# Retention on one NeuronCore: chunks of 64 tokens on 64x64 array tiles in place of chunks of 128, with the states formed one excursion ahead

## The chip, the cores and the metric

The kernel runs on one NeuronCore of a Trainium2 chip. The metric is the device time of one launch in microseconds. TensorE multiplies (a stationary operand is loaded, a moving one streams through a 128x128 array, and the result lands in PSUM), VectorE and ScalarE work on elements, GpSimd (POOL) and SyncE (SP) here mostly issue DMA transfers. Engines run side by side and wait for each other by semaphores; each works through its own instructions in order.

## The reference

Three stages follow each other. Retention is causal attention without softmax: for 8 batches, 8 heads, 576 tokens and 64 dimensions

```python
scores = scale * np.matmul(q, k.transpose(0, 1, 3, 2))
Dmat = np.where(rel >= 0, gamma[:, None, None] ** rel[None, :, :], 0.0)
return np.matmul(scores * Dmat[None], v)
```

where `rel` is the query's position less the key's and `gamma` is a constant per head. The heads are then joined to 4608 tokens of 512 features. The first expert layer ("moe") computes `((x @ w1) * (x @ w2)) @ w3 @ w_out`, the second ("moe2") computes `h = x @ w_in`, `g = h * clip(h + 3, 0, 6) / 6` and `g @ w_out`.

## The kernel before

**Products.** The expert layers use fp32r operands split into a high and a low part, three matmuls for each product (`mm3`, lines 124 to 128). The retention products and the product `w3 @ w_out` are plain fp32 matmuls; the trace shows each of these as two passes, with two weight loads and two matmuls. 

**Order.** The program is written as one long list of TensorE work, and everything else is put into it by slots: `at(s, f)` files a function under slot `s`, and `tick()`, called once before each `mm3` (or each weights product in the prologue), runs what is filed under the present slot. So the order of every queue, SP's and POOL's DMA issues among them, is the order of slots. `LEAD` is 14 slots, `B0 = LEAD + 64` is the first slot of the first expert layer, `SPB` = 96 slots is one block of 512 tokens there, and `E0` is the first slot of its last block.

**Stages.** The prologue (line 462 on) forms `W = w3 @ w_out` in 64 matmuls while SP loads the weights, whose 64-bit words VectorE and ScalarE turn into fp32 (`weights`, line 133). Then nine blocks `ffn1(j)` (line 497) compute the first expert layer: `pa`, `pb`, their product `ab`, and `px` from `ab` and `W`. Their output is stored to DRAM (`xod`) as the operands of a Strassen-like scheme, and the weights of moe2 are prepared meanwhile and stored to `wid` and `wqd` (`job`, line 608). In the second part `run_set` (line 744) multiplies `xod` operands by eight weight sets `wset` and writes the gated result to `gd`, and `out_block` (line 902) multiplies sums of `gd` blocks (`s_sum`, `prep`) by `wqd` weights and stores the output.

**Retention.** Its 36 tiles of 128 tokens (two heads side by side on the partitions, four head pairs) are woven into the prologue and the `ffn1` blocks as excursions: at slot `ex[t]` TensorE leaves the expert layer and runs `excursion(t)` (line 294): the scores of tile t+1, then for tile t the product of the queries with the state (`cross`), masked scores times values (`pv`), and this tile's addition to the state (`state`). A sequence is 4.5 tiles, so t % 9 decides where a state starts or ends: with t % 9 == 0 there is no cross product, with 4 it covers 64 queries, and with 8 no state is formed.

- `scores` (209): 16 matmuls on 64x64 array tiles, each with 64 keys as stationary operand; 8 stream 128 queries and 8 the later 64 alone.
- `cross` (225): 8 matmuls on 64x64 array tiles, 128 queries streamed (64 where t % 9 == 4), into the PSUM tile `z`.
- `pv` (240): 8 matmuls with 128 keys on the rows and 64 columns, 128 queries streamed, added to `z`.
- `state` (250): 8 matmuls with 128 keys on the rows and 64 columns, 64 streamed.

After it, at `ex[t] + 1`, VectorE scales the result (`x_out`, 270), adds the state to `S` in SBUF (`s_add`, 263) and masks the next scores (`p_mask`, 217, two instructions, one of two masks); `x_hi` and `x_lo` follow at +2 and +3, with `v_scale(t+1)` (200), and POOL issues `load_kv(t+2)` (194, three transfers) and `load_qk(t+3)`. A `kv` tile's buffer is one of two, and is filled again when `pv` and `state` have read it.

**The join.** In the last `ffn1` block SP loads operands (`load_xop`, 653) and the first weight sets (`load_set`, 642) into space that the first layer has left: sets 0, 1 and 2 at slots `E0` + 62, 76 and 88, set 3 at +105, after the last stores of `xod` (`x2_store`, 591, on SP in this block).

Of the kernel before, what the change touches and what calls it, by code (L numbers as in the profile page):

```python
# [26 lines left out]
def retention_moe_kernel(  # L27
# [54 lines left out]
    wqd = dram_p.tile([7, NSET, 128, 2, 256], F32, name="wqd")  # L82
# [125 lines left out]

    def scores(t):
        c = tiles[t]  # L210
        for a in range(2):
            for g, jh in ((0, 0), (0, 1), (1, 0), (1, 1)):
                for b, rows in enumerate(HALF):
                    nc.tensor.matmul(out=sc[HALF[jh ^ g], b, 2 * g + a, 64 * jh:128], lhsT=c["kT"][rows, g, a, HALF[jh]],  # L214
                                     rhs=c["q"][rows, g, a, 64 * jh:128], start=True, stop=True, skip_group_check=True)

    def p_mask(t):
        c = tiles[t]
        c["P"] = pl_p.tile([128, 2, NPAIR, 128], F32, tag="P", name="P")
        m = mask[:, 1 if t % PER == 4 else 0].rearrange("p g (o i) -> p g o i", o=1).to_broadcast([128, 2, 2, 128])  # L220
        for b in range(2):
            nc.vector.tensor_tensor(out=c["P"][:, b].rearrange("p (g a) i -> p g a i", g=2),
                                    in0=sc[:, b].rearrange("p (g a) i -> p g a i", g=2), in1=m, op=ALU.mult)

    def cross(t):
        c = tiles[t]
        zs = ps_z.tile([128, 2, 512], F32, tag="z", name="z")
        c["z"] = z = zs[:, :, 0:256].rearrange("p b (g i) -> p b g i", g=2)
        c["st"] = zs[:, :, 256:384].rearrange("p g (a e) -> p g a e", a=2)
        r = t % PER  # L230
        c["ni"] = ni = 0 if r == 0 else (64 if r == 4 else 128)
        if not ni:
            return
        for g in range(2):
            for a, cols in enumerate(HALF):
                for b, rows in enumerate(HALF):
                    nc.tensor.matmul(out=z[cols, b, g, 0:ni], lhsT=S[rows, 1 - g, a, :], rhs=c["q"][rows, g, a, 0:ni],
                                     start=g == 0, stop=False, skip_group_check=True)

    def pv(t):  # L240
        c = tiles[t]
        for g in range(2):
            for b in range(2):
                for a, cols in enumerate(HALF):
                    d = slice(128 * b + 64 * a, 128 * b + 64 * a + 64)
                    nc.tensor.matmul(out=c["z"][cols, b, g, :], lhsT=c["v"][:, g, d], rhs=c["P"][:, b, 2 * g + a, :],  # L246
                                     start=not c["ni"] and g == 0, stop=True, skip_group_check=True)


    def state(t):  # L250
        r = t % PER
        if r == 8:
            return
        c = tiles[t]
        for g in range(2):
            rows = HALF[1 - g] if r == 4 else slice(0, 128)
            for a in range(2):
                for b, cols in enumerate(HALF):
                    d = slice(128 * b + 64 * a, 128 * b + 64 * a + 64)
                    nc.tensor.matmul(out=c["st"][cols, 1 - g, a, :], lhsT=c["k"][rows, g, d], rhs=c["v"][rows, g, d],  # L260
                                     start=False, stop=True, skip_group_check=True)

    def s_add(t):
        c = tiles[t]
        if t % PER in (0, 4):
            nc.vector.tensor_copy(out=S, in_=c["st"])
        elif t % PER != 8:
            nc.vector.tensor_tensor(out=S, in0=S, in1=c["st"], op=ALU.add)

    def x_out(t):  # L270
# [3 lines left out]
        for a in range(0, 128, min(128, SEQ - off)):  # L274
            n, m = min(128, SEQ - off), (off + a) % SEQ // 64
            for p in range(NPAIR):
                nc.vector.scalar_tensor_tensor(
                    out=c["x32"][:, p, a:a + n], in0=c["z"][:, p % 2, p // 2, a:a + n], scalar=cw[:, m, p:p + 1],
# [27 lines left out]
    with tc.manual_schedule():  # L306
# [20 lines left out]
        mask = tb_p.tile([128, 2, 2, 128], F32, name="mask")  # L327
        sc = ps_sc.tile([128, 2, NPAIR, 128], F32, name="sc")
        nc.vector.memset(sc, 0.0)
        rate = tb_p.tile([128, PER, 8], F32, name="rate")  # L330
        cw = tb_p.tile([128, PER, NPAIR], F32, name="cw")
        S = tb_p.tile([128, 2, 2, 64], F32, name="S")
# [19 lines left out]
        mt = ut_p.tile([128, 2, 128], F32, name="mt")  # L352

        def load_tables():
            nc.vector.memset(g64[:, 0:1], 0.0)
            nc.gpsimd.dma_start(out=g64, in_=rates[64, 0:8].partition_broadcast(128))
            for g, rows, js in ((0, slice(0, 128), slice(0, 128)), (1, A, Bh), (1, Bh, A)):
                nc.gpsimd.dma_start(out=mt[rows, g], in_=tables[js, 0, 1, 0])
                nc.gpsimd.dma_start(out=back[rows, 4 * g:4 * g + 4], in_=rates[js, 4 * g:4 * g + 4])
# [662 lines left out]
```

## Time and profile before

| | |
|---|---|
| runs before (3) | 1465.98 us median, 1464.68 to 1471.44 |
| the profiled execution's own time | 1472.47 us |
| its span, first to last instruction | 1470.7 us |
| instructions | 24250 |
| busy share PE, DVE, ACT, POOL | 99%, 68%, 39%, 17% |
| DMA | 287.22 MB, mean 195 GB/s |

The profile is of one execution. PE is TensorE's matmuls, PEld its weight loads, DVE VectorE, ACT ScalarE; a name such as `z<-P,kv` gives the tile written and the tiles read, and L246 is line 246. Matmuls overlap, so a row's duration is longer than the time by which it moves the next one; the starts tell that.

### The profile page before, as it was taken

To read this page: it belongs to the slowest core of one execution; us is meant where nothing else is said; L and a number is where in the kernel's file an instruction comes from. 1 tells how busy PE (TensorE), PEld (TensorE's weight loads), DVE (VectorE), ACT (ScalarE), POOL (GpSimd) and SP (SyncE) were. 2 spreads that over 40 slices of the span, in tenths; PEclk is the share of its full clock that TensorE was granted. 3 is DMA by queue.
4 is the path that set the end of the run, shared out by engine and by line. 5 is a ranking of instruction groups with operands and counts; after the bars stand their busy time and mean duration, and the time that the engine had idled before them with its cause. 6 is when DMAs were issued, how large, how long until landed. Compare 5 with 4: busy or idle time off the path is not lost.

```text
span 1470.7 us, 24250 instructions
## 1 busy us (share of the span) xinstructions
PE 1460.6 (99%) x9536; PEld 1259.0 (86%) x9536; DVE 1006.0 (68%) x1725; ACT 570.0 (39%) x857; POOL 255.0 (17%) x471
## 2 busy tenths in 40 slices
PE   9999999999999999999999999999999999999998
PEld 5578888888888888888889999999998888888887
DVE  6986566566564746474545666666678888888887
ACT  6572333233333333242433333333344343343333
POOL 3413222222221122210002222222321000000000
PEclk9999999999999999999999999999999999999999
DMA  9963657565555655646689754635599444445441
GB/s 323 275 188 100 202 171 200 173 184 189 167 191 147 207 165 181 191 151 189 202 303 423 285 186 179 258 141 225 200 382 325 125 121 124 137 143 144 142 126 48
DMA packets 192723, 287.22 MB, mean 195 GB/s; under 512 B 12528, under 2 KB 143600, under 8 KB 192608
## 3 DMA queue, kind: packets, MB, share of 16 engines
q1 hardware_dynamic: 109728, 151.01, 31.1%
q0 software_dynamic: 25856, 75.93, 16.4%
q10 hardware_dynamic: 57024, 58.73, 11.9%
q8 instruction: 75, 1.23, 0.3%
q14 instruction: 40, 0.33, 0.1%
HBM read 176.04 MB, written 109.58 MB: 194 GB/s over the span
## 4 chain that ended last, share of the span: by engine, by line
PE 94%; DMA 4%; ACT 1%; DVE 0%; issue 0%; SPq 0%
PE pb L947 16%; PE pb L126 12%; PE pb L128 12%; PE pb L127 12%; PE pb L948 8%; PE px L126 5%; PE pa L126 5%; PE px L128 4%; PE pa L128 4%; PE px L127 4%; PE pa L127 4%; PE z L246 2%; DMA wr<-in_w_dram 2%; PE sc L214 2%; DMA wset<-wid 1%; PE Wps L468 1%
## 5 line engine op out<-in xcount | busy, mean ns | idle before, releaser
L947 PE MATMUL pb<-wq,op 128*128 128x512 f32 x1008 | 356.0, 399 | 0.3 <-issue 0.3
L948 PE MATMUL pb<-wq,op 128*128 128x256 f32 x1008 | 283.1, 281 | 0.0
L947 PEld LDWEIGHTS pb<-wq,op 128*128 128x128 f32 x1008 | 189.4, 188 | 47.6 <-issue 0.6
L126 PE MATMUL pb<-xop,wset 128*128 128x384 f32 x672 | 225.6, 336 | 2.3 <-DMA wset<-wid 2.1
L128 PE MATMUL pb<-xop,wset 128*128 128x384 f32 x672 | 225.9, 336 | 0.0
L127 PE MATMUL pb<-xop,wset 128*128 128x384 f32 x672 | 225.6, 336 | 0.0
L863 ACT CAST op<-unit 128x1024 fp32r<-128x1024 f32 x126 | 132.3, 1051 | 177.2 <-DVE unit L849 146.5
L948 PEld LDWEIGHTS pb<-wq,op 128*128 128x128 f32 x1008 | 190.5, 189 | 0.0
L131 DVE TENSOR_TENSOR op<-unit,op 128x1024 fp32r<-128x1024 f32 x126 | 153.9, 1222 | 31.0 <-ACT op L863 31.0
L197 POOL DMA_DIRECT2D kv<-in_kv_dram x108 | 58.9, 549 | 471.9 <-PE z L260 423.8
L126 PEld LDWEIGHTS pb<-xop,wset 128*128 128x128 f32 x672 | 126.2, 188 | 3.1 <-DMA wset<-wid 2.4
L127 PEld LDWEIGHTS pb<-xop,wset 128*128 128x128 f32 x672 | 126.2, 188 | 0.0
L128 PEld LDWEIGHTS pb<-xop,wset 128*128 128x128 f32 x672 | 126.2, 188 | 0.0
L126 PE MATMUL pa<-xh,w1h 128*128 128x512 f32 x288 | 114.2, 396 | 0.0
L126 PE MATMUL px<-abh,Wh 128*128 128x512 f32 x288 | 114.0, 396 | 0.0
L126 PE MATMUL pb<-xh,w2h 128*128 128x512 f32 x288 | 112.3, 390 | 0.0
L128 PE MATMUL px<-abh,Wl 128*128 128x512 f32 x288 | 112.2, 390 | 0.0
L128 PE MATMUL pa<-xh,w1l 128*128 128x512 f32 x288 | 112.2, 390 | 0.0
L128 PE MATMUL pb<-xh,w2l 128*128 128x512 f32 x288 | 112.2, 390 | 0.0
L127 PE MATMUL px<-abl,Wh 128*128 128x512 f32 x288 | 112.2, 389 | 0.0
L127 PE MATMUL pa<-xl,w1h 128*128 128x512 f32 x288 | 112.1, 389 | 0.0
L127 PE MATMUL pb<-xl,w2h 128*128 128x512 f32 x288 | 112.1, 389 | 0.0
(144 smaller groups left out, 2360.9 us busy)
## 6 DMA issues: line engine op xcount, KB each, us to landing
unit<-gd SPq DMA_DIRECT2D x72, 512.0 KB, 5.6
xop<-xod SPq DMA_DIRECT2D x42, 768.0 KB, 9.2
gd<-g POOLq DMA_DIRECT2D x122, 192.0 KB, 5.1
qk<-in_qk_dram POOLq DMA_DIRECT2D x144, 128.0 KB, 4.0
wset<-wid SPq DMA_DIRECT2D x8, 1792.0 KB, 17.7
gd<-gw POOLq DMA_DIRECT2D x70, 192.0 KB, 4.2
wr<-in_w_dram SPq DMA_DIRECT2D x24, 512.0 KB, 13.5
kv<-in_kv_dram POOLq DMA_DIRECT2D x36, 256.0 KB, 3.9
```

The costliest lines, as they stand in the source:

```text
L126: nc.tensor.matmul(out=out_ap, lhsT=sh, rhs=mh, start=first, stop=False, **kw)
L127: nc.tensor.matmul(out=out_ap, lhsT=sh, rhs=ml, start=False, stop=False, **kw)
L128: nc.tensor.matmul(out=out_ap, lhsT=sl, rhs=mh, start=False, stop=last, **kw)
L131: eng.tensor_tensor(out=out_ap, in0=x, in1=y, op=ALU.subtract)
L197: nc.gpsimd.dma_start(out=y[rows, g], in_=kv[2 * t + g, js].rearrange("j x h d -> j x (h d)"))
L214: nc.tensor.matmul(out=sc[HALF[jh ^ g], b, 2 * g + a, 64 * jh:128], lhsT=c["kT"][rows, g, a, HALF[jh]], rhs=c["q"][rows, g, a, 64 * jh:128 ...
L246: nc.tensor.matmul(out=c["z"][cols, b, g, :], lhsT=c["v"][:, g, d], rhs=c["P"][:, b, 2 * g + a, :], start=not c["ni"] and g == 0, stop=Tru ...
L468: nc.tensor.matmul(out=ps, lhsT=w3f[:, n // 4 % 8, n % 4 * 128:n % 4 * 128 + 128], rhs=wo[:, j, :], start=j == 0, stop=j == KF - 1)
L863: nc.scalar.copy(out=op_tiles(7 * b + p)[0], in_=src())
L947: nc.tensor.matmul(out=c[k], lhsT=h[:, ts], rhs=w, start=first and kt == 0, stop=False, skip_group_check=True)
L948: nc.tensor.matmul(out=c[k][:, 0:256], lhsT=l[:, ts], rhs=w[:, 0:256], start=False, stop=kt == 7, skip_group_check=True)
```

## The change

Chunks are now 64 tokens, two per tile, and every product runs on 64x64 array tiles with 64 columns streamed (`quarter`). `scores` has 16 quarters, with keys and queries of the same chunk. `cross` runs for each chunk that is not the first of its sequence, with its own state (three state buffers `X` in rotation), 8 quarters each. `pv` has 16 quarters into a PSUM region of its own, separate from that of `cross`. `state` has 16 quarters, or 8 where one chunk is the last of its sequence; it writes the second half of the scores' PSUM tile and is run one excursion ahead, right after the scores. So `p_mask` is one instruction, `s_add` two; a new `z_copy` (ScalarE) takes `pv`'s result out of PSUM and a new `z_sum` (VectorE) adds `cross`'s. `v_scale` and the `kv` loads move ahead accordingly, and `load_kv` is one transfer. In the prologue the excursions come 3 slots earlier from tile 0 on, the tables' loads later, and the load of the last `w_out` piece behind those of `w3`.

Apart from retention, sets 1 and 2 are loaded at slots `E0` + 70 and 80 (set 2 with a small ScalarE write in place of GpSimd's), `wqd` has its partitions ahead of the sets, `q_tile` issues four transfers in place of one, and in `out_block` the loads of the next block come in another order, with the late `wq` loads of block 0 among them, and the sums `s_sum` are filed ahead of `prep`.

```diff
-    wqd = dram_p.tile([7, NSET, 128, 2, 256], F32, name="wqd")
+    wqd = dram_p.tile([7, 128, NSET, 2, 256], F32, name="wqd")
...
     def load_kv(t):
-        y = raw_p.tile([128, 2, 2, 256], F32, tag="kv", name="kv", bufs=2)
-        for g, rows, js in ((0, slice(0, 128), slice(0, 128)), (1, A, Bh), (1, Bh, A)):
-            nc.gpsimd.dma_start(out=y[rows, g], in_=kv[2 * t + g, js].rearrange("j x h d -> j x (h d)"))
+        y = ut_p.tile([128, 2, 2, 256], F32, tag=f"kv{t}", name="kv") if t in (2, 3) else raw_p.tile([128, 2, 2, 256], F32, tag="kv", name="kv", bufs=2)
+        nc.gpsimd.dma_start(out=y.rearrange("j g x n -> j g (x n)"), in_=kv[2 * t:2 * t + 2].rearrange("g j x h d -> j g (x h d)"))
...
+    def chunk(t, h):
+        return (2 * t + h) % 9, X[(2 * t + h) % 3], X[(2 * t + h + 1) % 3]
+
+    def quarter(out_ap, lhsT, rhs):
+        nc.tensor.matmul(out=out_ap, lhsT=lhsT, rhs=rhs, start=True, stop=True, skip_group_check=True)
...
+        for g in range(2):
+            for a in range(2):
+                for h, keys in enumerate(HALF):
+                    for b, rows in enumerate(HALF):
+                        quarter(sc[keys, b, 0, 2 * g + a, :], c["kT"][rows, g, a, keys], c["q"][rows, g, a, keys])
...
+        c["P"] = pl_p.tile([128, 2, NPAIR, 64], F32, tag="P", name="P")
+        m = mask.rearrange("p (b q i) -> p b q i", b=1, q=1).to_broadcast([128, 2, NPAIR, 64])
+        nc.vector.tensor_tensor(out=c["P"], in0=sc[:, :, 0], in1=m, op=ALU.mult)
...
+    def state(t):
+        c = tiles[t]
+        for g in range(2):
+            for a in range(2):
+                for h, rows in enumerate(HALF):
+                    if chunk(t, h)[0] == 8:
+                        continue
+                    for b, cols in enumerate(HALF):
+                        d = slice(128 * b + 64 * a, 128 * b + 64 * a + 64)
+                        quarter(sc[cols, h, 1, 2 * g + a, :], c["k"][rows, g, d], c["v"][rows, g, d])
+
+    def s_add(t):
+        for h in range(2):
+            m, old, new = chunk(t, h)
+            if m == 0:
+                nc.vector.tensor_copy(out=new, in_=sc[:, h, 1])
+            elif m < 8:
+                nc.vector.tensor_tensor(out=new, in0=old, in1=sc[:, h, 1], op=ALU.add)
...
+        for h, i in enumerate(HALF):
+            m, S, _ = chunk(t, h)
+            if m == 0:
+                continue
+            for g in range(2):
+                for a, cols in enumerate(HALF):
+                    for b, rows in enumerate(HALF):
+                        quarter(c["zs"][cols, b, g, i], S[rows, 2 * g + a, :], c["q"][rows, g, a, i])
...
+                for h, rows in enumerate(HALF):
+                    for a, cols in enumerate(HALF):
+                        d = slice(128 * b + 64 * a, 128 * b + 64 * a + 64)
+                        quarter(c["zp"][cols, 2 * g + b, h, :], c["v"][rows, g, d], c["P"][rows, b, 2 * g + a, :])
+
+    def z_copy(t):
...
+        nc.scalar.copy(out=c["z"].rearrange("p q (h i) -> p q h i", h=2), in_=c["zp"])
+
+    def z_sum(t):
...
+        nc.vector.tensor_tensor(out=z, in0=z, in1=c["zs"][:, :, :, i], op=ALU.add)
...
             scores(t + 1)
+            if t >= 0:
+                state(t + 1)
         if t >= 0:
             cross(t)
             pv(t)
-            state(t)
...
-        at(LEAD - 4, load_tables)
+        at(LEAD + 10, load_tables)
...
-        at(LEAD + 33, lambda: load_qk(2))
+        at(LEAD + 33, lambda: (load_kv(2), load_qk(2)))
+        at(LEAD + 38, lambda: load_kv(3))
...
-        ex = {-1: LEAD + 34, 0: LEAD + 43, 1: LEAD + 48, 2: LEAD + 53, 3: LEAD + 58, 4: B0 + 52, 5: B0 + 63, 6: B0 + 74, 7: B0 + 85}
+        ex = {-1: LEAD + 34, 0: LEAD + 40, 1: LEAD + 45, 2: LEAD + 50, 3: LEAD + 55, 4: B0 + 52, 5: B0 + 63, 6: B0 + 74, 7: B0 + 85}
...
-                at(ex[t] + 1, lambda t=t: (x_out(t), s_add(t)))
+                at(ex[t] + 1, lambda t=t: z_copy(t))
+                if t + 1 < NTI:
+                    at(ex[t] + 1, lambda t=t: (p_mask(t + 1), s_add(t + 1)))
+                if t < 3:
+                    at(ex[t] + 1, lambda t=t: v_scale(t + 2))
+                at(ex[t] + 1, lambda t=t: (z_sum(t), x_out(t)))
...
+            if 2 < t < NTI - 2:
+                at(max(ex[t] + 3, ex[t + 1] - 9), lambda t=t: v_scale(t + 2))
+        at(LEAD + 36, lambda: v_scale(0))
+        at(ex[-1] + 1, lambda: p_mask(0))
+        at(LEAD + 39, lambda: state(0))
+        at(LEAD + 39, lambda: s_add(0))
+        at(LEAD + 38, lambda: v_scale(1))
...
-        for n, (t, s) in enumerate((("A1", 62), ("B1", 76), ("A2", 88), ("s4", 105), ("s5", 107), ("B2", 112), ("s6", 119), ("s7", 133))):
+        for n, (t, s) in enumerate((("A1", 62), ("B1", 70), ("A2", 80), ("s4", 105), ("s5", 107), ("B2", 112), ("s6", 119), ("s7", 133))):
...
                 if p == 0:
-                    for part in PARTS[:3]:
-                        at(now[0], lambda part=part: load_raw(b + 1, *part))
+                    loads = [lambda part=part: load_raw(b + 1, *part) for part in (PARTS[2], PARTS[0], PARTS[1])]
                     if b == 0:
-                        at(now[0] + 1, lambda: q_late(3))
+                        q = q_late(3)
+                        loads = loads[:2] + q[:1] + loads[2:] + q[1:]
+                    for f in loads:
+                        at(now[0], f)
```

## Rows read from the trace of the kernel before

**Rows 1.** The page, part 1: busy time, share of the span and instructions.
```profile
PE 1460.6 (99%) x9536; PEld 1259.0 (86%) x9536; DVE 1006.0 (68%) x1725; ACT 570.0 (39%) x857; POOL 255.0 (17%) x471
```

**Rows 2.** Waits of TensorE over the span: total us, times, longest.
```profile
PE pb L126 <- DMA wset<-wid: 2.1, 1, 2.1
PE Wps L468 <- DVE w3f L159: 0.6, 1, 0.6
PE sc L214 <- DMA qk<-in_qk_dram: 0.5, 1, 0.5
```

**Rows 3.** Timeline of TensorE, a regular excursion: start us, us, instructions.
```profile
204.21 0.90 PE L214 MATMUL sc<-qk 64*64 64x128 f32 x32
204.93 0.62 PE L237 MATMUL z<-qk,S 64*64 64x128 f32 x16
205.48 1.09 PE L246 MATMUL z<-P,kv 128*64 128x128 f32 x16
206.40 0.64 PE L260 MATMUL z<-kv 128*64 128x64 f32 x16
206.97 0.50 PE L126 MATMUL px<-abh,Wh 128*128 128x512 f32 x1
```

**Rows 4.** Timeline of TensorE, the excursion of a tile with t % 9 == 4.
```profile
262.13 0.90 PE L214 MATMUL sc<-qk 64*64 64x128 f32 x32
262.85 0.41 PE L237 MATMUL z<-qk,S 64*64 64x64 f32 x16
263.19 1.09 PE L246 MATMUL z<-P,kv 128*64 128x128 f32 x16
...
264.62 0.50 PE L126 MATMUL pa<-xh,w1h 128*128 128x512 f32 x1
```

**Rows 5.** Timeline of TensorE, the excursion of a tile with t % 9 == 0.
```profile
185.33 0.90 PE L214 MATMUL sc<-qk 64*64 64x128 f32 x32
...
187.65 0.50 PE L126 MATMUL pa<-xh,w1h 128*128 128x512 f32 x1
```

**Rows 6.** Windows, L237 alone: us, PE busy (matmuls running), PEclk, DMA share, GB/s.
```profile
262.85:262.90 0.06, 0.05 (x4) 1.00 0.00 0
...
263.02:263.08 0.06, 0.06 (x16) 1.00 0.00 0
```

**Rows 7.** Groups of instructions by line and form: xcount | busy us, mean ns.
```profile
L222 DVE TENSOR_TENSOR P<-sc,mask 128x512 f32<-128x512 f32 x72 | 46.1, 681 | 0.0
...
L268 DVE TENSOR_TENSOR S<-S,z 128x256 f32<-128x256 f32 x24 | 9.8, 410 | 0.0
...
L514 ACT COPY a<-pa 128x512 f32<-128x512 f32 x72 | 41.8, 581 | 31.4 <-PE pa L128 31.3
```

**Rows 8.** Windows: us, PE, PEld, DVE, ACT, POOL busy, PEclk, DMA, GB/s.
```profile
150.00:690.00 540.00, 540.00 (x4132) 445.15 (x4131) 316.74 (x597) 186.05 (x281) 104.21 (x190) 1.00 0.58 180
54.00:82.00 28.00, 27.32 (x290) 16.62 (x289) 27.18 (x52) 17.05 (x29) 12.30 (x22) 1.00 0.92 251
```

**Rows 9.** Timeline of the prologue, VectorE and TensorE.
```profile
46.47 0.68 DVE L203 TENSOR_TENSOR kv<-kv,rate 128x512 f32<-128x512 f32 x1
...
47.55 0.90 PE L214 MATMUL sc<-qk 64*64 64x128 f32 x32
...
49.87 4.56 PE L468 MATMUL Wps<-wo,w3f 128*128 128x512 f32 x10
```

**Rows 10.** Timeline of SP's DMA queue at the join.
```profile
755.60 1.36 SPq L646 DMA_DIRECT2D wset<-wid  x1
759.77 1.62 SPq L597 DMA_DIRECT2D xod<-x2l  x2
```

**Rows 11.** Windows at the join, columns as in rows 8.
```profile
745.00:756.00 11.00, 11.00 (x50) 9.13 (x49) 4.09 (x8) 3.74 (x6) 0.00 (x0) 1.00 0.43 150
761.50:780.40 18.90, 16.80 (x96) 16.30 (x95) 12.50 (x24) 7.41 (x13) 5.45 (x10) 1.00 1.03 399
```

**Rows 12.** The page, part 6: DMA issues, KB each, median us to landing.
```profile
unit<-gd SPq DMA_DIRECT2D x72, 512.0 KB, 5.6
```

More of the change, by code (lines that the diff above doesn't have):

```diff
@@ L217, in p_mask @@
     def p_mask(t):
         c = tiles[t]
[L219 to L223, printed above, removed]
+        c["P"] = pl_p.tile([128, 2, NPAIR, 64], F32, tag="P", name="P")
@@ L230, in cross @@
[L230 to L238, printed above, removed]
+        z = ps_z.tile([128, 2, 512], F32, tag="z", name="z")
@@ L243, in pv @@
             for b in range(2):
[L244 to L253, printed above, removed]
-        c = tiles[t]
[L255 to L263, printed above, removed]
+                for h, rows in enumerate(HALF):
[3 more added lines that the diff above has]
+    def z_copy(t):
+        c = tiles[t]
+        c["z"] = pl_p.tile([128, NPAIR, 128], F32, tag="zp", name="zp")
+        nc.scalar.copy(out=c["z"].rearrange("p q (h i) -> p q h i", h=2), in_=c["zp"])
+    def z_sum(t):
         c = tiles[t]
[L265 to L268, printed above, removed]
+        m = [chunk(t, h)[0] for h in range(2)]
+        i = slice(0 if m[0] else 64, 128 if m[1] else 64)
+        z = c["z"].rearrange("p (g b) i -> p b g i", b=2)[:, :, :, i]
+        nc.vector.tensor_tensor(out=z, in0=z, in1=c["zs"][:, :, :, i], op=ALU.add)
     def x_out(t):
@@ L277, in x_out @@
                 nc.vector.scalar_tensor_tensor(
-                    out=c["x32"][:, p, a:a + n], in0=c["z"][:, p % 2, p // 2, a:a + n], scalar=cw[:, m, p:p + 1],
+                    out=c["x32"][:, p, a:a + n], in0=c["z"][:, p, a:a + n], scalar=cw[:, m, p:p + 1],
                     in1=ut[:, p, 0:n], op0=ALU.mult, op1=ALU.mult)
@@ L326, in retention_moe_kernel @@
             nc.gpsimd.memset(x, 0)
-        mask = tb_p.tile([128, 2, 2, 128], F32, name="mask")
-        sc = ps_sc.tile([128, 2, NPAIR, 128], F32, name="sc")
-        nc.vector.memset(sc, 0.0)
+        mask = tb_p.tile([128, 64], F32, name="mask")
+        sc = ps_sc.tile([128, 2, 2, NPAIR, 64], F32, name="sc")
         rate = tb_p.tile([128, PER, 8], F32, name="rate")
         cw = tb_p.tile([128, PER, NPAIR], F32, name="cw")
-        S = tb_p.tile([128, 2, 2, 64], F32, name="S")
+        X = [tb_p.tile([128, NPAIR, 64], F32, tag=f"S{i}", name="S") for i in range(3)]
         x_tiles = {}
@@ L351, in retention_moe_kernel @@
         g64 = ut_p.tile([128, 8], F32, name="g64")
-        mt = ut_p.tile([128, 2, 128], F32, name="mt")
+        mt = ut_p.tile([128, 64], F32, name="mt")
         def load_tables():
@@ L356, in load_tables @@
             nc.gpsimd.dma_start(out=g64, in_=rates[64, 0:8].partition_broadcast(128))
-            for g, rows, js in ((0, slice(0, 128), slice(0, 128)), (1, A, Bh), (1, Bh, A)):
-                nc.gpsimd.dma_start(out=mt[rows, g], in_=tables[js, 0, 1, 0])
-                nc.gpsimd.dma_start(out=back[rows, 4 * g:4 * g + 4], in_=rates[js, 4 * g:4 * g + 4])
+            nc.gpsimd.dma_start(out=back, in_=rates[0:128, 0:8])
             for a, rows in enumerate(HALF):
+                nc.gpsimd.dma_start(out=mt[rows], in_=tables[A, 0, 1, 0, 0:64])
                 nc.gpsimd.dma_start(out=ut[rows].rearrange("q (g b) i -> q g b i", g=2),
@@ L372, in make_rates @@
             nc.vector.tensor_scalar(
-                out=mask[:, 0], in0=mt, scalar1=0.0, scalar2=None, op0=ALU.is_gt)
-            nc.vector.tensor_copy(out=mask[:, 1], in_=mask[:, 0])
-            for g, rows in enumerate(HALF):
-                nc.vector.memset(mask[rows, 1, g, 64:128], 0.0)
+                out=mask, in0=mt, scalar1=0.0, scalar2=None, op0=ALU.is_gt)
             parts = [(slice(0, 128), slice(r, r + 4), slice(e, e + 7, 2), slice(0, 8)) for r, e in ((0, 2), (5, 3))]
-            parts += [(HALF[jh ^ g], slice(4, 5), slice(e, e + 1), slice(4 * g, 4 * g + 4))
-                      for g in range(2) for jh, e in ((0, 10), (1, 1))]
+            parts += [(HALF[jh], slice(4, 5), slice(e, e + 1), slice(0, 8)) for jh, e in ((0, 10), (1, 1))]
             for rows, rs, es, hs in parts:
@@ L643, in load_set @@
             wset[n] = w = pool.tile([128, 2, 7 * 256], F32R, tag=tag, name="wset")
-            if n < 3:
+            if n == 2:
+                nc.scalar.copy(out=w[:, 0, 0:1], in_=half)
+            elif n < 2:
                 nc.gpsimd.memset(w.bitcast(F32)[:, 0, 0:1], 0.0)
@@ L801, in q_unit @@
             tq[p, u] = dst
-            nc.sync.dma_start(out=dst.bitcast(F32).rearrange("p (k n) -> p k n", k=2),
-                              in_=wqd[POS[p], 2 * u:2 * u + 2].rearrange("k p h n -> p k (h n)"))
+            nc.sync.dma_start(out=dst.bitcast(F32), in_=wqd[POS[p], :, 2 * u:2 * u + 2].rearrange("p k h n -> p (k h n)"))
         def q_tile(p):
@@ L807, in q_tile @@
             for u in range(4):
-                tq[p, u] = w[:, u]
-            nc.sync.dma_start(out=w.bitcast(F32).rearrange("p u (k n) -> p (u k) n", k=2),
-                              in_=wqd[POS[p]].rearrange("k p h n -> p k (h n)"))
+                q_unit(p, u, w[:, u])
         def q_late(i):
             w = ap["xl"].tile([128, 3, 1024], F32R, tag=f"s{4 + i}", name="wq")
-            for v in range(3):
-                q_unit(4 + (3 * i + v) // 4, (3 * i + v) % 4, w[:, v])
+            return [lambda v=v: q_unit(4 + (3 * i + v) // 4, (3 * i + v) % 4, w[:, v]) for v in range(3)]
         RAW = (9, 10, 0, 3, 4, 7, 8)
@@ L898, in retention_moe_kernel @@
                     if k > 4:
-                        q_late(k - 5)
+                        for f in q_late(k - 5):
+                            f()
         pending.pop()()
```

27 lines of the change are left out of this document (10 added, 17 removed).

## The prediction

> **What bounds the kernel now.** I read the page first, then the waits of TensorE, its timeline around single excursions, and last the prologue and the join of the two expert layers. The page has PE busy for 99% of the span, against 68% for VectorE and 39% for ScalarE [rows 1]. Busy time alone would prove little, so the waits decide: past the start TensorE waited 2.1 us for one `wset` load, 0.6 us for a conversion and 0.5 us for a `qk` load, and hardly elsewhere [rows 2]. So a microsecond of matmul that goes is a microsecond of the end, unless a new wait takes it, and what counts is how long each excursion into retention holds TensorE.
>
> The timeline gives that by the starts of the phases. A regular excursion (204.21 to 206.97) is scores 0.72, cross 0.55, pv 0.92, state 0.57, together 2.76 us [rows 3]. A tile with t % 9 == 4 takes 2.49 [rows 4], one with 0 takes 2.32 [rows 5], and one with 8, which has no state, 2.76 - 0.57 + 0.10 (the change back to the full array, below) = 2.29. Nine tiles take 6 x 2.76 + 2.49 + 2.32 + 2.29 = 23.66 us, all 36 take 94.6.
>
> **The price of a quarter.** Each fp32 matmul shows as two passes: 16 score matmuls, x32. If the four 64x64 quadrants work side by side, the price is the columns of one quadrant. Scores give each quadrant 2 x (128 + 64) = 384 columns, twice: 12 steps of 64 columns in 0.72 us, 0.060 us a step with the first fill. The short cross product of t % 9 == 4 (four passes to each quadrant, 64 columns) shows it bare: four more passes have begun in each 58 ns [rows 6]. Comparing the two cross products, 0.55 against 0.34 for four steps less, gives 0.0525. I take 0.060, from the longest run of quarters, and keep 0.0525 for the range.
>
> **The new excursion.** Scores no longer cross from one chunk to the next: 8 steps in place of 12. Cross keeps 8. pv now has 64 keys on each row half and 64 queries: 8 steps in place of 8 pairs of 128 columns, which took 0.92. State keeps 8. So 32 steps, 1.92 us, plus the change back to the full array, 0.57 - 8 x 0.058 = 0.10 [rows 3]: 2.02 in place of 2.76. Of nine tiles' 18 chunks two need no cross (4 steps each); two need no state, but the other half there has only two quadrants, so nothing is saved. 9 x 32 - 8 = 280 steps, 16.8 + 0.9 = 17.7 us, against 23.66: 5.96 less in nine tiles, 23.8 in 36. Of this the four tiles of the prologue have 0.54 + 3 x 0.74 = 2.8, and the other 32 have **21.0**.
>
> **What comes in beside it.** Each tile gets a ScalarE copy of 512 columns out of PSUM (0.58, as L514) and a VectorE sum of that size (0.68, as L222). One of the two mask products goes (0.68), and the state is added in two halves of 256 columns (2 x 0.41 for 0.41) [rows 7]. VectorE gains 0.41 and ScalarE 0.58 us per tile. From 150 to 690 us VectorE is busy 316.7 of 540 us and ScalarE 186.1, with TensorE granted its full clock, the 2.4 GHz level [rows 8]; excursions lie some 19 us apart [rows 3, 5], so this costs nothing there. If it were exposed it would be at most 1 us a tile. Two of three `kv` issues go from POOL, which has slack.
>
> **The prologue.** There the cover is gone: from 54 to 82 us VectorE is busy 27.18 of 28 [rows 8]. Over it the change adds four sums (2.7), takes five masks (3.4), adds 2.05 of state sums and drops some small table work, a mask copy of 256 columns (0.41 at most, by L268) and a few shorter steps, which I estimate at 1.0: 0.4 more. The first state also moves ahead of the first excursion and waits for `v_scale(0)`, which VectorE begins at 46.47 today, behind the tables. Five slots of weights product took 4.56 us, 0.91 each; four of them before the present 47.55 is 43.9 [rows 9], while `v_scale(0)`, with one mask product and 1.0 of tables less ahead of it, ends near 45.5. I take no gain of the 2.8 and **+0.4**; bounds: the whole 2.8 gained, or 1.6 lost to that wait and the 0.4 besides. The loads of tiles 2 and 3 move ahead of the conversions of w1, and the tables and one `w_out` piece behind w3; bytes stay, so I price the order at nothing, up to the 0.5 of the `qk` wait either way.
>
> **The join.** TensorE waits 2.1 us for a `wset` [rows 2], the fourth, which it needs after three sets of products. SP issues it behind the third, at 755.60, and two stores [rows 10]. From 745 to 756 us the DMA engines are 43% busy, from 761.5 to 780.4 full [rows 11]. That third set moves from slot 88 to 80, ahead of SP's wait for the `xod` stores, and so into the empty stretch: 1.8 MB leave the crowded one, some 4.5 us at its 399 GB/s. **-2.1**; nothing if the buffer comes free late.
>
> **moe2.** `wqd` is laid out so that a load reads 4 KB pieces, not 2 KB; stores keep 1 KB. The big load becomes four issues on SP, off TensorE's path. In the out blocks three loads and two sums change order, with nothing added; none of the waits of [rows 2] lies there. Priced at nothing; a load that came late would cost about its landing, 5.6 us, once [rows 12].
>
> **Sum.** -21.0 - 2.1 + 0.4 = -22.7 us. The profiled execution took 1472.47, so it would take 1449.8. The median of the runs is 1465.98, 6.5 below the profiled one, and no row says where that lies; the change moves both alike: **1443.3 us**.
>
> **Rivals.** *Feeding* (0.14): 64 matmuls follow each other where 40 did, and no row shows 64 at 29 ns each; the eight short cross ones did, the 16 of scores took 45. At 37 ns a nine takes 544 x 0.037 + 0.9 = 21.0, 2.6 less than now, 9.3 over 32 tiles: 1465.98 - 9.3 - 2.1 + 0.4 = 1455.0.
>
> *A fixed price per pass* (0.08), the other side: if a pass costs the same however few its columns, halving columns and doubling passes loses. State's 16 passes took 0.46, 29 ns each; scores 22.5. At the middle, 25.8 ns, nine tiles' 1088 passes take 28.1 + 0.9 = 29.0 us, 5.3 more, 19 over 32 tiles: 1483. It decides from 2.66 / 128 = 21 ns a pass in a regular tile. Against it stand the 16 passes in 0.23 us [rows 6], 14.6 ns each, though that is a short run.
>
> The Trainium skill speaks for this rival: TensorE: Matmul & The Clock Gate, section "Wait — 56ns, not 53.3ns?", has starts never closer than about 25 ns however few the columns. By that rule an excursion of 128 passes would take 3.2 us, an estimate, and the kernel would be slower. The trace doesn't agree for passes in different quadrants: they began 14.6 ns apart.
>
> *New waits* (0.08): the prologue loses 2.0, the `wset` wait stays and one load comes late in the out blocks, 5.6: -21.0 + 2.0 + 5.6 = -13.4, 1452.6. For it: full VectorE and DMA early on. Against: no wait elsewhere.
>
> *It doesn't bring what it takes out* (0.04): what TensorE saves between excursions returns as waits for VectorE or DMA: 1466. Against it: both are at 58 to 59% there [rows 8].
>
> **The numbers.** The forecast has 0.66. Low end: 0.055 a step gives 7.4 in nine tiles, 26 in the 32; with 2.1 and half of the prologue's gain, 1436. High end: past the middle of *feeding* and all of *new waits*, 1459; what is left out is the slow side and the rest of *feeding*. Half a per cent, 7.3 us, is about what a measurement here can tell from no change. Faster by more: 0.66 + 0.08 + 0.10 of *feeding*, 0.84. Within: 0.08. Slower: 0.08.
>
> **What would show it.** A regular excursion of about 2.0 us, four phases of 0.48 with no gap between cross and pv; no wait for `wset`; VectorE still full to about 80 us, and the expert layer's first matmul about when it comes now. I am wrong if an excursion takes over 2.3 us, if TensorE waits for the summed or scaled tiles between excursions, or if the out blocks show waits for `unit` or `wq`.

## The result, and the profile after

The changed kernel takes 1450.91 us (median of 4 runs, 1450.39 to 1451.26), the kernel before, beside it, 1468.71 (4 runs, 1464.68 to 1473.28). The ratio is 0.9866, 95% interval 0.9839 to 0.9892: faster, by 17.8 us, inside the forecast's range but short of its 22.7. The profiled executions took 1472.47 us before and 1450.39 after.

The page of the changed kernel, its part 1 and the granted clock of part 2, against [rows 1]:

```profile
PE 1433.4 (99%) x11136; PEld 1240.5 (86%) x11136; DVE 1021.4 (71%) x1751; ACT 583.5 (40%) x894; POOL 222.9 (15%) x395
...
PEclk9999999999999999999999999999999999999999
```

PE has 1600 more matmuls and is busy 27 us less. The granted clock reads nine tenths or more in every slice of the page; a fall for 3.41 us, which slices of 36 us don't show, follows below. Its waits past the start, against [rows 2]:

```profile
PE sc L212 <- DVE S L245: 3.2, 2, 3.0
PE sc L212 <- DVE kv L202: 2.3, 2, 1.6
...
PE pb L128 <- DVE w2l L131: 1.7, 2, 1.1
PE pa L127 <- DVE xl L131: 1.3, 1, 1.3
```

The wait for `wset` is gone. In its place stand four groups, 8.5 us together, all for VectorE. The timeline of TensorE (start us, us, instruction) shows a regular excursion, as [rows 3] did, and the two places where the prologue now stops:

```profile
44.80 0.69 PE L212 MATMUL sc<-kv 64*64 64x64 f32 x32 [1.57 <-DVE kv L202]
45.42 1.12 PE L485 MATMUL Wps<-wo,w3f 128*128 128x512 f32 x2
49.51 1.13 PE L212 MATMUL sc<-qk 64*64 64x64 f32 x32 [2.96 <-DVE S L245]
...
80.76 0.58 PE L126 MATMUL pa<-xh,w1h 128*128 128x512 f32 x1
82.64 0.50 PE L127 MATMUL pa<-xl,w1h 128*128 128x512 f32 x1 [1.31 <-DVE xl L131]
...
208.11 0.69 PE L212 MATMUL sc<-qk 64*64 64x64 f32 x32
208.63 0.65 PE L212 MATMUL sc<-kv 64*64 64x64 f32 x32
209.09 0.65 PE L212 MATMUL z<-qk,S 64*64 64x64 f32 x32
209.56 0.65 PE L212 MATMUL z<-P,kv 64*64 64x64 f32 x32
...
210.14 0.50 PE L126 MATMUL px<-abh,Wh 128*128 128x512 f32 x1
```

Scores 0.52, state 0.46, cross 0.47, pv and the change back 0.58: 2.03 us in place of 2.76, with no gap between them. The single starts in the trace show how: the four passes of a group, one on each quadrant, begin within 20 ns, and the next group begins 58 ns after the first.

The excursion at 49.51 is slower, 3.20 us, where an undisturbed one with t % 9 == 0 takes 1.79. The windows of the two, with the granted clock third from the end, tell why:

```profile
49.30:52.60 3.30, 3.09 (x112) 3.08 (x112) 0.16 (x1) 0.00 (x0) 1.05 (x2) 0.50 1.04 264
208.00:210.00 2.00, 2.00 (x129) 1.89 (x128) 0.69 (x1) 0.00 (x0) 0.00 (x0) 1.00 1.02 333
```

From 49.26 on, at the end of TensorE's stop of 2.96 us, the granted clock is 0.50, the 1.2 GHz level, for 3.41 us; the kernel before has no such fall. It costs 1.4 us here. The starts of the timeline's rows divide each execution into stages. "Changed, again" is a second profiled execution of the same code (below), "best" the fastest variant:

| us | before | changed | changed, again | best |
|---|---|---|---|---|
| excursion of tile 4 starts | 114.02 | 119.51 | 120.47 | 116.29 |
| sum of the 32 excursions of tiles 4 to 35 | 83.3 | 63.15 | 62.21 | 62.8 |
| last excursion ends | 685.89 | 672.35 | 672.10 | 668.53 |
| first product of `run_set` | 756.75 | 743.21 | 742.96 | 739.39 |
| from there to the first out block | 353.4 | 350.9 | 350.9 | 350.9 |
| out blocks, first to last product | 356.3 | 350.0 | 356.0 | 350.0 |
| span | 1470.7 | 1448.6 | 1454.4 | 1444.8 |

So between the profiled spans 22.1 us lie: 13.5 before `run_set` (19.0 gained from tile 4 on, 5.5 lost ahead of it), 2.5 in `run_set`, and 6.3 in the out blocks, where nothing was expected; 0.2 are lost again behind the last product. "Changed, again" has the same fall of the clock (3.41 us from 50.79, behind a stop of 3.73), "best" has none.

### The profile page after: what moved, and what is told of

Its sections match the earlier page's. It is cut to its first block, busy times and chain, and to the rows that moved or that the text cites. A ratio compares the mean times of both kernels' runs of the same rounds, so it can differ in the third digit from the quotient of the medians.

```text
span 1448.6 us, 27406 instructions
## 1 busy us (share of the span) xinstructions
PE 1433.4 (99%) x11136; PEld 1240.5 (86%) x11136; DVE 1021.4 (71%) x1751; ACT 583.5 (40%) x894; POOL 222.9 (15%) x395
## 4 chain that ended last, share of the span: by engine, by line
PE 89%; DVE 5%; DMA 4%; issue 1%; ACT 1%; POOL 0%; SPq 0%; ACTq 0%; DVEq 0%
PE pb L967 15%; PE pb L128 12%; PE pb L126 12%; PE pb L127 12%; PE pb L968 7%; PE px L126 4%; PE pa L126 4%; PE px L128 4%; PE px L127 4%; PE pa L128 4%; PE pa L127 4%; PE sc L212 2%; PE z L212 2%; DMA wr<-in_w_dram 1%; DMA kv<-in_kv_dram 1%
## 5 line engine op out<-in xcount | busy, mean ns | idle before, releaser
L967 PE MATMUL pb<-wq,op 128*128 128x512 f32 x1008 | 349.7, 393 | 0.2 <-DVE stg L723 0.2
L968 PE MATMUL pb<-wq,op 128*128 128x256 f32 x1008 | 279.6, 277 | 0.0
L196 POOL DMA_DIRECT2D kv<-in_kv_dram x36 | 26.2, 727 | 482.4 <-PE z L212 475.5
## 6 DMA issues: line engine op xcount, KB each, us to landing
wset<-wid SPq DMA_DIRECT2D x8, 1792.0 KB, 15.4
```

What stands on the lines that cost most here:

```text
L196: nc.gpsimd.dma_start(out=y.rearrange("j g x n -> j g (x n)"), in_=kv[2 * t:2 * t + 2].rearrange("g j x h d -> j g (x h d)"))
L967: nc.tensor.matmul(out=c[k], lhsT=h[:, ts], rhs=w, start=first and kt == 0, stop=False, skip_group_check=True)
L968: nc.tensor.matmul(out=c[k][:, 0:256], lhsT=l[:, ts], rhs=w[:, 0:256], start=False, stop=kt == 7, skip_group_check=True)
```

## The experiments

Theory at the outset: the excursions and the join do what was forecast, the prologue loses to VectorE's order, and the out blocks' 6.3 us are no work of the edits (theory) or of the new order there (rival).

**The kernel before, once more.**

> The kernel before once more, unchanged, for its out blocks. In the profiled execution of before each out block of 112 matmuls took 19.79 us, in that of after 19.41, 18 blocks, 6.4 us in all. Theory A (the pace belongs to the moe2 edits): 19.8 here too, time 1464 to 1473 us. Theory B (the pace changes from execution to execution): it may be 19.4, and then the time is near 1465; a time near 1472 goes with 19.8.

It took 1472.04 us; its out blocks 356.3 again, 19.79 each from the second on. Its `wset` wait is 1.5 us, and `run_set` takes 352.7, 0.7 less than in the first execution: so far apart are two executions of one code there. The 17 runs of before in that batch fall into two groups, 8 at 1463.3 to 1466.5 and 9 at 1470.3 to 1476.7.

**Only the edits outside retention**, on the kernel before:

```diff
-("B1", 76), ("A2", 88)
+("B1", 70), ("A2", 80)
-    wqd = dram_p.tile([7, NSET, 128, 2, 256], F32, name="wqd")
+    wqd = dram_p.tile([7, 128, NSET, 2, 256], F32, name="wqd")
...
```

> The kernel before with only the moe2 part of the change (layout of wqd, order of loads and sums, slots of the weight sets); retention and prologue as before. Theory A: the out blocks take 19.4 us each and the wset wait is gone, so 2.1 + 6.4 = 8.5 us less than the executions of before that run at 19.8. Theory B: only the 2.1 us of the wset wait, against a before at the same pace of its out blocks. Both: excursions of 2.76 us as before.

1469.69 us (10 runs, 1464.54 to 1475.93), ratio 1.001, interval 0.9986 to 1.0035: alone they gain nothing that these runs could tell from no change. The wait for the fourth set is gone, but at the join TensorE still stops, at another place. The first line is VectorE's timeline of the kernel before, the others are VectorE's, ScalarE's and TensorE's of this run:

```profile
751.08 0.42 DVE L131 TENSOR_TENSOR stg<-x 128x256 f32<-128x256 f32 x1 [13.77 <-DMA wqd<-stg]
...
754.19 0.43 DVE L131 TENSOR_TENSOR stg<-x 128x256 f32<-128x256 f32 x1 [17.52 <-DMA wqd<-stg]
...
761.24 0.48 ACT L754 COPY stghi<-pb 128x384 f32<-128x384 f32 x1 [0.39 <-DMA xod<-stghi]
...
759.06 0.34 PE L128 MATMUL pb<-xop,wset 128*128 128x384 f32 x1
761.82 0.42 PE L126 MATMUL pb<-xop,wset 128*128 128x384 f32 x1 [2.42 <-issue]
```

VectorE waits 17.5 us for the buffer of a `wqd` store, 3.75 more than before, and what it forms for `xod` comes as much later. ScalarE's copy out of `pb` waits for that store of `xod`, and TensorE goes on 0.1 us after the copy; its row names no releaser. Behind the stop the granted clock is 0.50 for 3.41 us, and `run_set` takes 354.7 in all. That the earlier set load delays the `wqd` store, by sharing the DMA engines, is likely but not shown: in the changed kernel, with the same slots, the wait for that store is 12.7. The out blocks ran 19.41 us each (the second 20.11) up to block 13 and 19.79 from there on, within one execution.

**The changed kernel with the old moe2 layout and order.**

```diff
-                    loads = [lambda part=part: load_raw(b + 1, *part) for part in (PARTS[2], PARTS[0], PARTS[1])]
+                    for part in PARTS[:3]:
+                        at(now[0], lambda part=part: load_raw(b + 1, *part))
...
```

> The kernel after with the layout of wqd and the loads and sums of the out blocks as before; the new slots of the weight sets stay. Theory A: out blocks of 19.8 us, time 1451 + 6.4 = 1457 us. Theory B: 19.4 us and 1451 us in most executions. Both: excursions of 2.025 us, no wset wait.

1457.09 us (4 runs, 1454.16 to 1459.02), ratio 0.9918, 0.9888 to 0.9949. Its out blocks take 356.3 (19.79 each), and `run_set` 350.9, so layout and order are not what removed the `wset` wait. Against "changed, again", which has nearly the same out blocks, its span (1457.2) is 2.8 longer, 2.6 of it already there at the first product of `run_set` (745.55): 1.0 at the start of tile 4, where none of these edits has acted and the clock is 0.50 for 6.83 us in place of 3.41, and 1.6 from there on, 1.0 of them in one excursion that takes 2.76 in place of 1.79, waiting 0.74 for a scaled `kv`.

**The first state earlier**, ahead of the scaling that waits for a load:

```diff
-        at(LEAD + 35, make_rates)
+        at(LEAD + 28, make_rates)
...
-        at(LEAD + 39, lambda: state(0))
-        at(LEAD + 39, lambda: s_add(0))
+        at(LEAD + 38, lambda: state(0))
+        at(LEAD + 38, lambda: s_add(0))
         at(LEAD + 38, lambda: v_scale(1))
```

> The kernel after with two moves in the prologue: the table arithmetic seven slots earlier on VectorE, and the first state with its sum one slot earlier, so that the sum stands ahead of the scaling that waits for a kv load. Theory: TensorE's waits of 1.6 and 3.0 us near 43 and 46 us are VectorE's order, not its work; both shrink, the first expert matmul comes 3 to 4 us earlier and the time is near 1447 us. Rival: VectorE has too much work up to 86 us, the waits move to the first expert block, and the time stays at 1451 us.

1452.47 us (6 runs: three at 1448.5 to 1450.0, three at 1454.9 to 1456.6). The time is the rival's, or close to it: the three lower runs average 1449.3, 1.4 below the five lower ones of the changed kernel (1450.6, in another batch). Its mechanism is not, for the waits did not move to the first expert block; they became DMA waits:

```profile
47.70 0.69 DVE L202 TENSOR_TENSOR kv<-kv,rate 128x512 f32<-128x512 f32 x1 [4.03 <-DMA kv<-in_kv_dram]
...
48.45 0.69 PE L212 MATMUL sc<-kv 64*64 64x64 f32 x32 [3.19 <-DVE kv L202]
```

`kv(1)` itself lands late, so the order on VectorE was only half of it. A second stop, 1.93 us for the `qk` load of tile 2, ends at 56.75, and the clock falls to 0.50 behind that one (3.41 us from 57.11).

**The same, with the first four loads of `w1` 12 slots later**, out of the way of `kv` and `qk`:

```diff
-... else LEAD + 26 + 4 * i, s - 4, None, piece(),
+... else LEAD + 38 + 4 * i, s - 4, None, piece(),
```

> x_early with the first four loads of w1 twelve slots later, behind the kv and qk loads of the first tiles. Theory: in x_early TensorE and VectorE waited for the kv load of tile 1 and the qk load of tile 2 (3.2 and 1.9 us of TensorE) because the DMA engines are full up to 60 us; without 2 MB of w1 ahead of them these waits go, VectorE starts its backlog earlier, and the first expert matmul comes about 4 us earlier than at 80.8 us; about 1446 us at the faster pace of the out blocks. Rival: VectorE's work from 50 to 88 us is the bound, or the later w1 loads make a wait of their own: the first expert block starts at 81 us as in after.

1451.2 us (4 runs, 1448.35 to 1454.2). The profiled one (1448.35) had out blocks of 19.41 as the changed kernel's, and `run_set` began at 741.17 in place of 743.21: half of what the theory expected.

**The order of the quadrants.** All quarters of one row half ahead of those of the other, so that only two quadrants are used in turn:

```diff
-        for g in range(2):
-            for a in range(2):
-                for h, keys in enumerate(HALF):
-                    for b, rows in enumerate(HALF):
+        for b, rows in enumerate(HALF):
+            for g in range(2):
+                for a in range(2):
+                    for h, keys in enumerate(HALF):
...
```

> The kernel after with the quarters of each product in another order: first all on one row half of the array, then all on the other, so that two quadrants work at a time and not four; the same 64 matmuls of 64 columns. Theory (the price is the columns of the busiest quadrant): 64 steps of 0.058 us and 0.1, a regular excursion of 3.8 us in place of 2.025, some 60 us more in all, near 1511 us. Rival (a fixed price per pass): 2.025 us and 1451 us as in after.

1465.82 us. Its timeline has the regular excursion from 210.70 to 213.25:

```profile
210.70 0.80 PE L212 MATMUL sc<-qk 64*64 64x64 f32 x26
211.29 0.27 PE L212 MATMUL sc<-kv 64*64 64x64 f32 x2
211.34 0.28 PE L212 MATMUL sc<-qk 64*64 64x64 f32 x3
...
213.25 0.50 PE L126 MATMUL px<-abh,Wh 128*128 128x512 f32 x1
```

2.55 us, which neither side expected: the loss is a quarter, not a factor of two. The rows between these show why: matmuls of the next phase (`sc<-kv`), on the first row half, start among the last of `sc<-qk`, on the second. So TensorE starts passes ahead of their place in the program where they use the other row half, and fills most of the gaps. The order of quadrants alone is worth some 15 of the 20 to 21 us that the excursions gained (their 32 sum to 77.9 here; one execution, with the out blocks of 350.0).

**Narrower quarters**, each as two matmuls of 32 columns, the same columns in all:

```diff
-        nc.tensor.matmul(out=out_ap, lhsT=lhsT, rhs=rhs, ...)
+        for i in range(0, 64, 32):
+            nc.tensor.matmul(out=out_ap[:, i:i + 32], lhsT=lhsT, rhs=rhs[:, i:i + 32], ...)
```

> The kernel after with each quarter split into two matmuls of 32 columns: the same columns, 256 passes in place of 128, and twice the weight loads. Theory (columns): 2.03 us for a regular excursion and 1451 us. Rival (after is already at the floor of 14.6 ns a pass, or at its weight loads): 256 x 0.0146 + 0.1 = 3.8 us for a regular excursion, some 60 us more.

1614.57 us. The first fence is its undisturbed regular excursion, the second its largest group of waits, the third one of these stops and the fourth, from the view of the DMA queues in the window of that stop, the queue that carries instructions (transfers, MB, share):

```profile
548.55 1.17 PE L213 MATMUL sc<-qk 64*64 64x32 f32 x63
...
552.56 0.50 PE L126 MATMUL px<-abh,Wh 128*128 128x512 f32 x1
```

```profile
PE z L213 <- issue: 46.8, 26, 3.6
```

```profile
368.49 0.72 PE L213 MATMUL z<-P,kv 64*64 64x32 f32 x35 [3.20 <-issue]
```

```profile
q8 instruction: 1, 0.02, 1.8%
```

256 passes took 4.01 us less 0.10 for the change back, 15.3 ns each; the 128 of the changed kernel (2.025 less 0.10) 15.0 ns each. A pass costs the same at 32 and at 64 columns: a group of four still begins 58 ns after the last in most places. And 256 in a row are more than TensorE is fed with: in many excursions it stopped for up to 3.6 us with nothing to wait for that the profile shows as a wait. Each of the eleven such stops of 2.4 us or more holds the start of a transfer of kind "instruction", 16 KB, that begins 0.2 to 1.4 us after TensorE has stopped, and TensorE goes on 1.23 to 1.57 us after it has landed. By these times they were stops for instructions; of the shorter ones several have no such transfer, and their cause stays open. At or behind stops the granted clock fell 16 times to 0.50, 78.5 us in all, so part of the 164 us that this run is longer is the clock and not the passes.

**The changed kernel with the old slots of sets 1 and 2.**

> The kernel after with the weight sets 1 and 2 loaded at slots E0 + 76 and 88 again (and GpSimd's write for set 2). Theory: TensorE waits 2 to 2.5 us for the fourth wset again, 1453 us at the faster pace of the out blocks. Rival: the wait of before came from another transfer, and went with the retention part: no wait, 1451 us.

1455.67 us (4 runs, 1452.81 to 1458.47). The wait is back, but short, and `run_set` takes 351.9 in place of 350.9:

```profile
765.96 0.34 PE L128 MATMUL pb<-xop,wset 128*128 128x384 f32 x1
767.03 0.45 PE L126 MATMUL pb<-xop,wset 128*128 128x384 f32 x1 [0.73 <-DMA wset<-wid]
```

Of the 2.5 us (1.8 against the second execution of before) the slots brought 1.0; the rest went with the old retention, and with the old retention the new slots brought nothing in sum. This execution starts `run_set` 1.6 us later (744.85): 0.8 of it is there at tile 4 (120.30), behind a wait for `S` of 3.53 in place of 2.96, and 0.9 comes after it, 0.4 of that in waits for `w2h` and `w2l` near 128 us.

**The changed kernel, the best variant and one more, on one chip.**

> The changed kernel, unchanged, once more. Theory (the two rhythms of the out blocks, 19.41 and 19.79 us each, belong to the execution and not to the code): its runs fall into two groups, near 1450.5 and near 1456.5, as those of the variants of it did, and the ratio to before lies near 0.987 to 0.989. Rival (the new order of loads and sums in the out blocks holds TensorE in the faster rhythm): all runs lie at 1450 to 1452 as its first four did, and the ratio is at or below 0.986.

1450.82 us (6 runs: five at 1449.86 to 1451.46, one at 1456.14), before 1470.36 beside it (11 runs), ratio 0.9878, 0.9857 to 0.9899. The one at 1456.14 is the profiled one. So identical code has both rhythms. The windows from 1200 to 1300 us (matmuls in brackets behind PE's busy time), first the kernel before, then the changed one's two executions:

```profile
1200.00:1300.00 100.00, 100.00 (x567) 86.69 (x566) 87.92 (x117) 40.14 (x47) 0.00 (x0) 1.00 0.47 132
```

```profile
1200.00:1300.00 100.00, 100.00 (x579) 87.40 (x578) 90.15 (x119) 39.29 (x46) 0.00 (x0) 1.00 0.49 137
```

```profile
1200.00:1300.00 100.00, 100.00 (x568) 86.71 (x567) 87.93 (x117) 39.79 (x46) 0.00 (x0) 1.00 0.47 133
```

579 against 567 or 568 matmuls in 100 us, at the same clock of 1.00 and with PE busy throughout. So the difference is no wait, and it needs no edit. The single starts tell more. In the first rhythm a matmul of 512 columns is followed after 230 to 233 ns and one of 256 after 112 to 118; in the second after 232 to 241 and 112 to 121. All 13 profiled executions begin their out blocks in the first, and the rhythm changes where the stream of matmuls is interrupted for a moment. With the old order that is once, at the 96th of the 112 matmuls of the first block, with a step of 615 to 622 ns to the next, and all three executions go on in the second rhythm. With the new order it is at the 17th matmul of the second block (384 to 510 ns) and at the 97th (305 to 310 ns), and of ten executions six go on in the first rhythm and four in the second. One of the six, the run with the edits outside retention alone, changed once more in block 13, at a step of 266 ns. No change lies elsewhere.

> The earlier state with four w1 loads 12 slots later, once more, beside the changed kernel on one chip. Theory (its profile lost 2.0 us less in the prologue): 2.0 us below the changed kernel in runs of the same rhythm, groups near 1448.4 and 1454.5. Rival (the four w1 loads come late elsewhere, or the earlier profile was a lucky execution): same groups as the changed kernel, within 0.5 us.

1448.35 us (6 runs: four at 1446.59 to 1448.78, two at 1453.73 and 1454.26), ratio to before 0.9867, 0.9843 to 0.989. The lower group's mean, 1447.7, is 2.9 below that of the changed kernel's five (1450.6), and no run of the one group lies within the other: the theory held. It is the code of the run above with the `w1` loads 12 slots later, whose profile had tile 4 at 117.94 and not at 116.29: so far apart are two executions of it in the prologue. Its timeline:

```profile
45.01 0.69 PE L212 MATMUL sc<-qk 64*64 64x64 f32 x32
46.38 0.69 PE L212 MATMUL sc<-kv 64*64 64x64 f32 x32 [0.68 <-DVE kv L202]
...
54.12 0.40 PE L212 MATMUL sc<-qk 64*64 64x64 f32 x11 [1.37 <-DMA qk<-in_qk_dram]
...
77.54 0.58 PE L126 MATMUL pa<-xh,w1h 128*128 128x512 f32 x1
79.42 0.50 PE L127 MATMUL pa<-xl,w1h 128*128 128x512 f32 x1 [1.30 <-DVE xl L131]
...
83.88 0.50 PE L128 MATMUL pb<-xh,w2l 128*128 128x512 f32 x1 [1.09 <-DVE w2l L131]
```

The stop of 2.96 us at 49.51 is one of 0.68, the clock does not fall, and the first expert matmul comes 3.2 us earlier. A wait of 1.37 for a `qk` load is new; the waits for `xl` and `w2l` stay. The wait for `xl` is VectorE's queue: from 47.84 to 79.4, where it finishes `xl`, VectorE pauses twice, 2.08 us for TensorE, which waited for that `qk` load, and 1.24 for ScalarE, and else never for 0.1 us.

> As the run before it, and besides GpSimd in place of VectorE takes the low parts of x of tiles 0 to 2 and the scaling of v of tiles 2 and 3, five operations of 0.69 us off VectorE between 54 and 77 us. Theory (what is left of the prologue's loss is VectorE's queue, continuously busy from 53 to 88 us): the waits of the first expert block for xl and w2l shrink, its first matmul comes up to 2 us earlier than the 79.2 us of the earlier profile, and the groups lie near 1446 to 1447 and 1452 to 1453. Rival (the DMA loads of w1 and w2 or the products of the weights set it, or GpSimd is so much slower that its results come later): no change, or the first expert matmul waits longer for xl.

1457.29 us (6 runs: two at 1451.86 and 1452.09, four at 1457.13 to 1458.32), each group some 4 us above that of the run before: the rival held. Its GpSimd and TensorE timelines:

```profile
72.53 2.21 POOL L131 TENSOR_TENSOR xl<-x,xh 128x512 fp32r<-128x512 f32 x1 [6.62 <-ACT xh L297]
...
82.06 0.47 PE L127 MATMUL pa<-xl,w1h 128*128 128x512 f32 x1 [1.46 <-DVE xl L131]
```

GpSimd took up to 2.21 us for what VectorE does in 0.68, and its next `kv` and `qk` issues stood behind it. The wait for `xl` did not shrink. So how much a lighter VectorE would bring there stays open: this run moved work to a queue that was itself on the path.

## Why the prediction was right, and where it was not

**The excursions: right.** Forecast 21.0 us from the 32 excursions behind the prologue; they sum to 83.3 before and 62.2 in "changed, again", 21.1 less. In the first execution they are 63.15, 20.2 less, for one of them (188.84) held a wait of 0.71 for the scaled `kv`, behind a VectorE operation of 2.03 us; the variants with the new order of quarters and 64 columns have that wait too, 0.24 to 0.75. It is one of the signs that the prediction named for being wrong, here worth less than 1 us. The regular one was put at 2.02 us and is 2.025; the step of 0.060 us per 64 columns of one quadrant held over 64 quarters (58 ns between the starts of groups). The stretch from tile 4 to the last excursion's end gained 19.0 and 20.2: beside that wait, one of 0.6 us for `w2l` near 127 us, and little else, came in.

**Feeding** was refuted at this size, 128 passes in 2.025 us; it is real at twice the passes (the stops of the narrow run, the long ones at instruction transfers). **A fixed price per pass** was right as a mechanism and wrong in its price: it is 58 ns on one quadrant, 15 ns across four, which lies below the 21 ns from which it would have decided. The Trainium skill, TensorE: Matmul & The Clock Gate, section "Wait — 56ns, not 53.3ns?", has starts never closer than about 25 ns. The traces here do not agree where the passes go to four quadrants: 15.0 ns at 64 columns, 15.3 at 32. That such a floor exists, independent of the columns, they do bear out between 32 and 64 columns, at 58 ns for each quadrant.

**The prologue: the step that failed.** "I take no gain of the 2.8 and +0.4", with 2.0 as the worst; it lost 5.5 (6.5 in "changed, again"). The wait of the first state for `v_scale(0)` was named at 1.6 and is 1.57. What was missed is the queue: `s_add(0)` stands on VectorE behind `v_scale(1)`, and that waits for the `kv(1)` load. VectorE's timeline of the changed kernel:

```profile
44.06 0.68 DVE L202 TENSOR_TENSOR kv<-kv,rate 128x512 f32<-128x512 f32 x1
46.65 0.69 DVE L202 TENSOR_TENSOR kv<-kv,rate 128x512 f32<-128x512 f32 x1 [1.91 <-DMA kv<-in_kv_dram]
47.26 0.68 DVE L155 SCALAR_TENSOR_TENSOR w3f<-w3f,sign 128x512 int32<-128x512 int32 x1
...
49.03 0.42 DVE L245 TENSOR_TENSOR S<-S,sc 128x256 f32<-128x256 f32 x1
52.84 0.69 DVE L226 TENSOR_TENSOR P<-sc,mask 128x512 f32<-128x512 f32 x1 [3.39 <-PE z L212]
```

VectorE idles 1.91 us for the load, converts two pieces, adds the state at 49.03, TensorE starts its next scores at 49.51, and VectorE idles 3.39 us for TensorE. Two engines wait for each other in turn, and 1.4 of the 3.39 are the excursion at half clock. From 52.84 to the end of `xl` at 82.6 VectorE pauses twice more, 0.40 and 1.25 us, so what it idled before comes out late at the end: the expert layer's first matmul comes 2.8 us later (77.94 to 80.76), waits 1.31 for `xl`, then 1.1 for `w2l`, 5.2 together, near the 5.3 that VectorE idled. That sums so close is in part chance, for the kernel before has a pause there too (1.49 us for ScalarE, ending at 54.45). The variants bear the mechanism out: the order alone moves the wait to the DMA, order and loads together take 1.6 and 3.2 us of the 5.5 away, part of it the clock that does not fall there. No run parts the clock from the waits. My text counted the operations on VectorE, and not who stands behind whom there, though it was I who noted that the state "waits for `v_scale(0)`".

**The join: right in sum, in part wrong in cause.** Forecast 2.1; `run_set` gained 2.5, or 1.8 against the second execution of before. The slots do take the wait for the fourth set away, as argued. But with the old retention another stop of 2.4 came in its place, and with the new they are worth 1.0.

**moe2: priced at nothing.** The changed kernel with the old layout and order loses nothing in `run_set`. In the out blocks its 356.3 are the second rhythm, which the changed kernel has too in one of two profiles. One thing is open: the profiled executions with the old order (three) all had 19.79 from the second block on, of ten with the new order five had 19.41 to the end. The order moves the interruptions at which the rhythm is settled, so it may shift the odds; three are too few to say.

**The base.** "No row says where that lies; the change moves both alike": the 6.5 us between the profiled execution and the median are as much as this rhythm makes (356.3 against 350.0 in the out blocks). In the last batch the changed kernel's five lower runs average 1450.6, the four lowest of before (1464.87 to 1466.16) 1465.35: 14.7 us. Its one upper run, 1456.14, stands against 1471.56, the mean of the six highest of before: 15.4; one run of before, 1468.44, lies between. So the change's own gain is some 15 us (about 21.1 + 2.5, less 5.5 to 6.5 in the prologue and 1 to 2 in small waits), and the 17.8 and 19.5 between the medians are more because the changed kernel fell into the quicker rhythm in 9 of 10 runs, by their times. Whether chance or the new order did that is open; the forecast did not have it. That before's lower group has that rhythm is inferred from the distance; none of its profiles caught it.

## What to carry to other kernels

Price small matmuls on array tiles by passes and by columns of one quadrant, measure at which width the two meet (here a pass is 58 ns on one quadrant, 15 ns across four, at 64 columns and at 32), and order them so that neighbours use different quadrants. When work moves ahead in time, write down for its consumer's engine which instruction stands in front and what that one waits for; counting busy time misses it. Look at the granted clock behind every stop of TensorE, in windows as short as the stop. Where runs of one kernel fall into two groups, find the stage that differs before a difference between two medians is put down to an edit.

## What the runs showed that was not expected

The out blocks run in one of two rhythms, at a granted clock of 1.00 and without a gap in PE: 112 matmuls take 19.41 or 19.79 us, 6 us over the 18 blocks, in identical code. In all 13 profiles a rhythm lasts until a short interruption of the matmuls and may change there; which one follows is not settled. TensorE starts passes of one row half out of the program's order while the other is busy (2.55 us where two quadrants were used at a time, and not the 3.8 that the theory had counted for the program's order). 256 short passes in a row outran its supply of instructions, 128 did not. And at stops of TensorE (1.9 to 4.1 us long in the runs with 64 columns) the granted clock fell to the 1.2 GHz level for 3.4 or 6.8 us, which cost the changed kernel's prologue 1.4 us more than the stop itself.
